# Moving the last transfer of a cached-attention decode kernel, and the wait for it, from SyncE to ScalarE

## The chip, the cores and the metric

The kernel runs on one core of one Trainium2 chip. The metric is device microseconds (us) of that core for one execution. Times of several executions are given as medians.

Each engine of the core runs its own program. In this kernel TensorE does the matmuls, VectorE and ScalarE the elementwise work, and SyncE nothing but issue transfers and wait; they wait for one another by counters, called semaphores. Its matmul results lie in PSUM, everything else that it keeps on the core in SBUF. The instruction that starts a transfer shows in the trace as its **issue slice**; the bytes move afterwards, in packets, through the 16 transfer (DMA) engines that the profile counts.

Two quantities are used beside the time: the **span**, which the profile gives for an execution (first recorded instruction to last), and the time less the span of the same execution, called **time past the span** below. The span is listed to 0.1 us for each run, so a single time past the span is good to 0.05 us only, and means carry more than single values.

## The reference

One token (x has 512 elements) goes through layer norm, attention over a cache of 65536 positions (32 query heads, 8 key/value heads of width 128), the output projection, then a gated feed-forward of width 1792.

```python
def _A_ref(x, k_cache, v_cache, wq, wo):
    q = (x @ wq).reshape(B, Sq, Hq, Dh)...          # cut
    scores = jnp.einsum("bhqd,bhkd->bhqk", q, k) * (Dh ** -0.5)
    p = _softmax(scores, axis=-1)
    o = jnp.einsum("bhqk,bhkd->bhqd", p, v)
    return o...reshape(B, Sq, Hq * Dh) @ wo         # cut

h  = x + _A_ref(_layernorm(x), A_k_cache, A_v_cache, A_wq, A_wo)
h2 = h + ((_sigmoid(g) * u) @ w_down)               # g, u from layernorm(h) @ w_gate, w_up
return h2                                           # 1 x 1 x 512, bfloat16
```

The two caches are 2 x 8 x 65536 x 128 bfloat16 elements, 268 MB of the 282 MB that are read. The output is one row of 1 KB.

## The kernel before

A small class records the instructions of each engine with what they depend on, gives each engine a semaphore, each stream of transfers another, and emits one program per engine. The parts that matter:

```python
def dma(self, eng, fn, sem, deps=(), name=None):      # a transfer adds 16 to its own semaphore when it has landed
    self.op(eng, fn, deps, name)
    ...

HINTED = ("pe", "dve", "act")    # these three programs lie in a loop that is never repeated
def hinted(e, eng):
    ...
    with self.nc.body(first, valid_engines=here):
        loc = eng.mark_branch_hint_location()
        run(e, eng)
        eng.br_lt(never, 1, on_true=first, on_false=end).branch_hint(loc)     # L189
    self.nc.switch_bb(end)

for e, eng in (("sp", nc.sync), ("pool", nc.gpsimd), ("act", nc.scalar), ("dve", nc.vector), ("pe", nc.tensor)):
    ...
    (hinted if e in HINTED else run)(e, eng)
    nc.br("fin", engines=here)                        # every engine leaves its own program here
nc.switch_bb("fin")
for sem, v, _ in (value[d] for d in self.at_end):
    nc.sync.wait_ge(sem, v)                           # L211: the last wait of the kernel
```

SyncE issues all loads but that of x, each when its place is free (for nearly all of them a slot in a ring of four of 4 MB). The last of them are the three pieces of w_down. Then comes the end:

```python
# 56 matmuls (L831) leave the output in PSUM, a quarter each on rows 0, 32, 64, 96 of one bank
for g in (0, 2, 1, 3):
    if g < 2:   # VectorE
        op("dve", lambda e, g=g: e.tensor_copy(y_sb[:, 128*g:128*g+128], ps(YB, 0, 128, 32*g, 32*g+1)), ["y"], f"ysb{g}")
    else:       # ScalarE
        op("act", lambda e, g=g: e.activation(y_sb[:, 128*g:128*g+128], ps(YB, 0, 128, 32*g, 32*g+1), AF.Copy), ["y"], f"ysb{g}")
dma("sp", lambda e: e.dma_start(out[0], y_sb[:, :]), "out", [f"ysb{g}" for g in range(4)], "out")    # L841
P.at_end = ("out",)
```

## Time and profile before

| | before |
|---|---|
| time, median | 658.1 us (3 runs); 658.24 with the 3 taken beside the changed kernel |
| span of the profiled execution | 657.1 us |
| read from HBM | 282.33 MB, 430 GB/s over the span |
| last matmul ends | 655.26 us |
| last copy of the output ends | 655.90 |
| output issued, packet moves, wait over | 655.96, 656.71, 657.10 |

The lines behind this table stand in the prediction. The table is read from the bottom up: a change of the last transfer can act on the 1.2 us after the last copy. Everything else is a stream of loads, and time that a transfer engine loses in the stream is lost at the end too (run j below measures it: 0.27 us for each of eight added packets of 0.31).

### The profile page before, as it was taken

To read this page: it belongs to the slowest core of one execution; us is meant where nothing else is said; L and a number is where in the kernel's file an instruction comes from. 1 tells how busy PE (TensorE), PEld (TensorE's weight loads), DVE (VectorE), ACT (ScalarE), POOL (GpSimd) and SP (SyncE) were. 2 spreads that over 40 slices of the span, in tenths; PEclk is the share of its full clock that TensorE was granted. 3 is DMA by queue.
4 is the path that set the end of the run, shared out by engine and by line. 5 is a ranking of instruction groups with operands and counts; after the bars stand their busy time and mean duration, and the time that the engine had idled before them with its cause. 6 is when DMAs were issued, how large, how long until landed. Compare 5 with 4: busy or idle time off the path is not lost. (4 is left out here: it accounts for less than half of the span.)

```text
span 657.1 us, 6111 instructions
## 1 busy us (share of the span) xinstructions
PE 420.5 (64%) x2315; PEld 74.1 (11%) x1547; DVE 349.7 (53%) x439; ACT 42.9 (7%) x114; POOL 3.6 (1%) x17
## 2 busy tenths in 40 slices
PE   0688488548666585576765575764866668556746
PEld 0200011011000010010100110101100001001322
DVE  2399775547537665347555374465743575542202
ACT  1100200020000200020000200002000100002001
POOL 1000000000000000000000000000000000000000
PEclk9989689677888697776966769765888869677676
DMA  9999999999999999999999999999999999999998
GB/s 383 447 433 429 439 423 431 431 447 415 447 415 447 437 425 447 415 447 419 443 441 421 447 415 447 423 439 443 419 447 415 447 427 435 445 417 427 435 430 352
DMA packets 10802, 282.34 MB, mean 430 GB/s; under 512 B 1329, under 2 KB 1330, under 8 KB 1842
## 3 DMA queue, kind: packets, MB, share of 16 engines
q1 hardware_dynamic: 10658, 282.33, 99.7%
q10 hardware_dynamic: 144, 0.00, 0.0%
HBM read 282.33 MB, written 0.00 MB: 430 GB/s over the span
## 5 line engine op out<-in xcount | busy, mean ns | idle before, releaser
L431 PE MATMUL PS<-ktw 128*128 128x512 bf16 x1024 | 299.9, 442 | 157.4 <-DVE ktw L511 153.6
L511 DVE STREAM_TRANSPOSE ktw<-ring 128x1024 f32<-128x1024 f32 x256 | 291.6, 1205 | 128.0 <-DMA ring<-in_A_k_cache_dram 128.0
L431 PE MATMUL PS<-ring,PT_sb 128*32 x1024 | 83.9, 455 | 23.6 <-issue 13.2
L431 PEld LDWEIGHTS PS<-ktw 128*128 x256 | 27.1, 106 | 408.2 <-issue 256.8
L565 DVE STREAM_TRANSPOSE PT_sb<-P_sb 128x512 bf16<-128x512 bf16 x32 | 20.2, 684 | 54.0 <-PE PS L602 52.3
L551 ACT ACTIVATE negmax<-PS 128x1 f32<-128x1 f32 x8 | 1.4, 171 | 520.6 <-PE PS L549 520.6
L431 PEld LDWEIGHTS PS<-ring,PT_sb 128*32 x1024 | 25.8, 116 | 79.8 <-issue 74.6
L516 DVE TENSOR_REDUCE M_sb<-PS 128x1 f32<-128x512 f32 x32 | 19.9, 684 | 25.5 <-PE PS L431 25.5
L555 ACT ACTIVATE P_sb<-PS,negmax 128x512 bf16<-128x512 f32 x32 | 21.6, 686 | 0.3
L572 DVE TENSOR_REDUCE lsum<-PS 128x1 f32<-128x4 f32 x8 | 1.3, 163 | 31.2 <-PE PS L570 31.2
L542 PE MATMUL PS<-identf,gm 128*1 128x128 f32 x16 | 3.4, 301 | 16.9 <-DVE gm L540 16.9
L616 DVE TENSOR_TENSOR Lw<-O,blk_of 128x896 bf16<-128x896 bf16 (+1 forms) x2 | 1.4, 683 | 20.6 <-ACT O L606 20.6
L402 PE MATMUL PS<-st,onesf 128*128 128x2 f32 x4 | 1.2, 362 | 16.1 <-DVE st L401 16.1
L431 PE MATMUL PS<-ring,xz 128*8 x32 | 9.2, 459 | 2.3 <-issue 2.3
L599 ACT ACTIVATE po_sb<-PS,rl 128x512 bf16<-128x512 f32 x8 | 5.5, 687 | 53.2 <-PE PS L431 53.2
L431 PE MATMUL PS<-ktw,O 128*1 x26 | 7.6, 464 | 0.0
L549 PE MATMUL PS<-one_f,gmrep 1*128 1x1 f32 x16 | 4.2, 330 | 5.0 <-DVE gmrep L546 5.0
L555 ACT ACTIVATION_READ_ACCUMULATOR P_sb<-PS,negmax 128x1 f32 x32 | 6.5, 202 | 0.0
L476 DVE STREAM_TRANSPOSE qt<-qh 32x512 bf16<-32x512 bf16 x1 | 0.7, 699 | 10.6 <-ACT qh L473 10.6
L602 PE MATMUL PS<-sel_bf,po_sb 128*128 128x4 bf16 x32 | 2.0, 168 | 6.4 <-ACT po_sb L599 6.4
L417 DVE CAST hT<-x_col 128x4 f32<-128x4 bf16 x1 | 0.2, 171 | 10.6 <-DMA x_col<-in_A_x_dram 10.6
L661 DVE COPY yr<-PS 1x512 f32<-1x512 f32 x1 | 0.7, 679 | 8.3 <-PE PS L659 8.3
(82 smaller groups left out, 74.0 us busy)
## 6 DMA issues: line engine op xcount, KB each, us to landing
ring<-in_A_k_cache_dram SPq DMA_DIRECT2D x32, 4096.0 KB, 28.7
ring<-in_A_v_cache_dram SPq DMA_DIRECT2D x31, 4096.0 KB, 26.4
ring<-in_A_wq_dram SPq DMA_DIRECT2D x1, 4096.0 KB, 12.3
ktw<-in_A_wo_dram SPq DMA_DIRECT2D x1, 3584.0 KB, 12.7
ring<-in_A_v_cache_dram SPq DMA_DIRECT2D x1, 3072.0 KB, 13.2
ring<-in_B_w_gate_dram SPq DMA_DIRECT2D x1, 1792.0 KB, 19.0
ring<-in_B_w_up_dram SPq DMA_DIRECT2D x1, 1344.0 KB, 21.7
ring<-in_A_v_cache_dram SPq DMA_DIRECT2D x1, 1024.0 KB, 15.2
```

Of the source, the lines that this page charges most:

```text
L431: return e.add_instruction(mybir.InstMatmult(name=nc.get_next_instruction_name(), engine=mybir.EngineType.PE, ins=[rhs, lhsT], outs=[e.low ...
L511: op("dve", lambda e, d=dst, sr=src: e.transpose(d, sr), deps, f"T{b}.{c}", to="T")
L516: op("dve", lambda e, u=u: e.tensor_reduce(M_sb[:, u % 4:u % 4 + 1], ps(u % NS, 0, 512), AX.X, ALU.max), [f"S{b}.{NC - NR + k}"], f"mx{u}" ...
L542: op("pe", lambda e: e.matmul(ps(MISC, 0, 128, 0, 1), lhsT=gm[:, :], rhs=identf[:, :], start=True, stop=True), [f"gm{h}"], f"gmT{h}", to="Q")
L549: op("pe", lambda e: e.matmul(ps(MISC, 128, 129), lhsT=gmrep[0:1, :], rhs=one_f[0:1, 0:1], start=True, stop=True), [f"gmrep{h}"], f"neg{h}")
L551: op("act", lambda e: e.activation(negmax[:, k:k + 1], ps(MISC, 128, 129), AF.Copy, scale=-att_scale), [f"neg{h}"], f"negmax{h}")
L555: op("act", lambda e, b=b: e.activation(P_sb[:, (b % 4) * 512:(b % 4 + 1) * 512], ps(b % NS, 0, 512), AF.Exp, bias=negmax[:, k:k + 1], sca ...
L565: op("dve", lambda e, b=b: e.transpose(PT_sb[:, (b % 4) * 512:(b % 4 + 1) * 512], P_sb[:, (b % 4) * 512:(b % 4 + 1) * 512]), [f"E{b}", f"o ...
L572: op("dve", lambda e: e.tensor_reduce(lsum[:, :], ps(MISC, 132, 136), AX.X, ALU.add), [f"l{h}"], f"ls{h}", to="D")
L599: op("act", lambda e: e.activation(po_sb[:, :], ps(PO, 0, 512), AF.Copy, scale=rl[:, :]), [f"PV{NR * h + NR - 1}", f"rl{h}"], f"po{h}", to ...
L602: op("pe", lambda e, t=t: e.matmul(ps(OX, 0, 4), lhsT=po_sb[:, t * 128:(t + 1) * 128], rhs=sel_bf[:, 8 * t:8 * t + 8:2], start=(t == 0), s ...
L616: op("dve", lambda e: e.tensor_tensor(Lw[i][:, :].rearrange("p (j c) -> p j c", j=n), bass.AP(tensor=O2, offset=j0, ap=[[NQ, 128], [1, n], ...
```

## The change

The intent: the engine that makes half of the last copies issues the transfer itself and waits for it, so that SyncE is not woken across engines at the very end.

```diff
         for sem, v, _ in (value[d] for d in self.at_end):
-            nc.sync.wait_ge(sem, v)
+            nc.scalar.wait_ge(sem, v)
...
-        dma("sp", lambda e: e.dma_start(out[0], y_sb[:, :]), "out", [f"ysb{g}" for g in range(4)], "out")
+        dma("act", lambda e: e.dma_start(out[0], y_sb[:, :]), "out", [f"ysb{g}" for g in range(4)], "out")
```

## The prediction

> **What bounds the kernel now.** I read the page of the profile from the top, then the chain of waits and the timeline of the last microseconds, then the waits of the queue that issues the transfers. The page first:
>
> ```profile
> span 657.1 us, 6111 instructions
> PE 420.5 (64%) x2315; PEld 74.1 (11%) x1547; DVE 349.7 (53%) x439; ACT 42.9 (7%) x114; POOL 3.6 (1%) x17
> DMA  9999999999999999999999999999999999999998
> DMA packets 10802, 282.34 MB, mean 430 GB/s; under 512 B 1329, under 2 KB 1330, under 8 KB 1842
> q1 hardware_dynamic: 10658, 282.33, 99.7%
> q10 hardware_dynamic: 144, 0.00, 0.0%
> ```
>
> The reader is to see that the DMA row is full from the first slice on (only the last, with the tail in it, has 8): 282.34 MB at 430 GB/s is 656.6 us, the span itself. No compute engine is above 64%. The kernel streams the two caches and the weights, and only what lies after the last byte has arrived is not streaming. All but a sliver goes through queue 1, fed by SyncE; queue 10 has 144 packets, which is the load of x issued by ScalarE (128 rows and 16 small packets more). The output goes through queue 1 now. So the change touches the last piece of the span and nothing of the stream; the share of ScalarE's busy time (7%) says nothing about it.
>
> The last piece is in the timeline of the end (columns: start us, us, engine, line, operation, tiles, count, idle time before and what ended it):
>
> ```profile
> 653.58 1.68 PE L831 MATMUL PS<-ring,hhT 128*1 128x128 bf16 x56 [0.98 <-DVE hhT L826]
> 655.31 0.57 ACT L839 ACTIVATE y_sb<-PS 1x128 bf16<-1x128 f32 x2 [4.23 <-PE PS L831]
> 655.31 0.59 DVE L837 CAST y_sb<-PS 1x128 bf16<-1x128 f32 x2 [1.78 <-PE PS L831]
> 655.96 0.33 SPq L841 DMA_DIRECT2D out_dram<-y_sb  x1
> ```
>
> and in the waits of SyncE's queue from 600 us on (columns: engine and line, what it waited for, total us, times, longest):
>
> ```profile
> SPq L120 <- ACT y_sb L839: 25.9, 1, 25.9
> SPq L365 <- PE PS L431: 14.8, 2, 8.0
> SPq L362 <- PE PS L431: 11.1, 1, 11.1
> SPq L211 <- DMA out_dram<-y_sb: 0.8, 1, 0.8
> ```
>
> Here one sees the whole tail. The last matmuls end at 655.26. ScalarE and VectorE each copy two quarters of the output row out of PSUM, to 655.88 and 655.90. SyncE has stood waiting for 25.9 us (so its last weight load was issued by about 630), issues the output at 655.96, is busy with the issue for 0.33, until 656.29, and waits 0.8 more, to 657.1, where the span ends. From the last copy to the end it is 657.1 - 655.90 = 1.2 us: 0.06 from the copy to the issue, 0.33 of issue, 0.8 of flight and receipt. That 1.2 us is 0.18% of the time, and it is the most that any form of this change could remove. In the records of the transfers the one packet of 1 KB moves at about 656.71, some 0.75 us after the issue starts, so about 0.4 us of the wait is the way back to the waiting engine.
>
> **What the Trainium skill says.** "DMA: Bandwidth & Descriptors", section "SWDGE vs HWDGE vs iDMA", states that a transfer issued by ScalarE takes the same hardware descriptor path as one issued by SyncE, and its section "Issuing engines are not separate DMA queues" that they end on the same 16 engines, so that another issuer saves only sequencer time. The trace of before agrees as far as it goes: the issue of x on ScalarE took 375 ns; SyncE's issues were 327 to 501 ns (median 328) for the K loads, 419 to 432 for the closely following w_down loads, 326 for the output. "Perfetto Trace Analysis", section "Per-engine timelines", says that data movement is outside the issue's slice and that a write to HBM can hold up the final semaphore; the 0.8 us of waiting after a 0.33 us slice, with no other traffic, agrees. "Runtime: NRT & Kernel Launch", section "The ~15µs preamble/postamble breakdown", gives about 5 us of barrier and reset after the kernel; the measured 658.1 is only 1.0 above the profiled span of 657.1 (two executions, so not exactly comparable), so that work can't all be in the metric. The same page, section "Instruction fetch mechanics", warns that a taken branch can stall on the fetch of its target. This I take up as a rival.
>
> **The change, part by part.**
>
> *The issue moves to ScalarE.* One instruction leaves SyncE's program and one enters ScalarE's. It still depends on the four copies. Two are ScalarE's own, two VectorE's. A copy's completion must still be waited for even by the engine that made it, since the transfer reads the bytes from SBUF: there is a semaphore wait either way. What might be gained is the hop from ScalarE to SyncE, but VectorE's copies end last (655.90 against 655.88) and their hop remains, to another listener. So the start of issue stays at about 655.96: at best 0.02 earlier, if the sequencer's waits are in another order 0.03 to 0.05 later.
>
> Is ScalarE's sequencer there in time? The records of its loop-closing branch say so: ScalarE ran the branch of L189 at 655.3, for 53 ns, while its copies were still to be executed. The sequencer runs ahead of its engine, so it will already be standing at the wait when the copies end, as SyncE does now.
>
> *The duration of the issue.* SyncE took 326 ns. ScalarE's only sample is 375, but it ran at 0.80 while SyncE was also issuing at 0.81, and SyncE's own closely spaced issues are slower too. Nobody else issues at the end. I take 326 to 375, thus 0 to +0.05 us.
>
> *Flight and receipt.* Same 1 KB, same single packet, same destination, all weight traffic over (the last of it at 654.6, with no more packets before the output's): 0.8 us, change 0. Queue 10 is empty, but so is queue 1 by then, so there's nothing to overtake.
>
> *ScalarE's branches.* After the issue ScalarE must run the compare-and-branch (53 ns) and a jump before it reaches the final wait. This lies beside the 0.8 us of flight: 0 on the path.
>
> *SyncE is freed.* It ends at about 630 instead of 657.1. It would only have waited; the stream of loads is issued in the same order at the same times. 0.
>
> Sum: -0.02 to +0.05 at the start, 0 to +0.05 in the issue, 0 in flight, 0 in the end wait: between -0.02 and +0.10 us of 658.1, some 0.015% at the most. Three runs of before span 0.16 us, so this is under the noise.
>
> **The rivals.**
>
> *The output is held up on ScalarE.* If the sequencer could not process the transfer until the engine's own queue is drained, or the branch to the common end block stalls on instruction fetch for longer than the 0.8 us of flight, the end moves later. For it: after the change the path out of ScalarE's hinted loop is on the engine that decides the end, before it was not. Against: the branch now takes 53 ns, and up to 0.8 us of any stall is hidden. It would make 658.4 to 659.5.
>
> *The hop is real and saved.* If most of the 0.06 us between copy and issue, and part of the 0.4 us on the way back to the waiter, belong to SyncE rather than to the memory, ScalarE may do both faster. For it: the change has one engine that copies, issues and waits. Against: half of the copies are on VectorE, and the way back comes from the transfer, whoever listens. It would make 657.8 to 658.0.
>
> *The end of the program has another order.* SyncE can reach the closing barrier 27 us early and ScalarE is last. If what is measured past the span (1.0 us) includes a hand-over from engine to engine, it may shift by a few tenths either way: 657.7 to 658.5. Nothing in the trace speaks to its sign.
>
> *The stream is disturbed.* No load changes issuer or order, and the queue's share is full in 39 of 40 slices. I give this nearly nothing. A whole-run shift of over 0.3% could only come from another state of the chip.
>
> **Range and chances.** The centre is 658.1, the old median plus about 0.03. The 80% range is the third rival's width, a little wider to the side of the first: 657.7 to 658.6. For 2% it would take 13.2 us, eleven times the whole 1.2 us tail: faster is excluded by the profile (0.005 is for the measurement), slower is nearly so (0.005, a bad state or an unforeseen stall).
>
> **What would show it.** In the changed profile the transfer should be in ScalarE's queue at 655.9 to 656.0 relative to a tail like this one (0.05 to 0.11 us after the last copy), 0.33 to 0.38 long, the end wait of L211 with ScalarE as the waiter and 0.7 to 0.9 us, and q10 with 146 packets, q1 two fewer (10656). The DMA row, 430 GB/s and the K and V issues unchanged. It would be wrong if the gap from last copy to issue grew beyond 0.2 us, if the issue lasted over 0.5, or if the end wait grew to over 1 us; a change in the time without any of these would be the third rival.

## The result, and the profile after

658.54 us (median of 6, 658.4 to 658.81) against 658.24 (6 runs, 658.04 to 658.39). The ratio is 1.0005, 95% interval 0.9993 to 1.0018: the same. A ratio compares the means of the runs of the two kernels, not the medians quoted beside it (the ratios come out when the first execution of each kernel, the profiled one, is left out).

The end of the changed kernel, as the timeline has it (start us, us, engine, line, operation, tiles, count, idle time before and what ended it), and after it the one line for the final wait (L211, by engine, with its duration in ns and its start):

```profile
655.07 0.34 PE L831 MATMUL PS<-ring,hhT 128*1 128x128 bf16 x8 [0.23 <-DMA ring<-in_B_w_down_dram]
655.45 0.59 DVE L837 CAST y_sb<-PS 1x128 bf16<-1x128 f32 x2 [1.71 <-PE PS L831]
655.45 0.56 ACT L839 ACTIVATE y_sb<-PS 1x128 bf16<-1x128 f32 x2 [3.96 <-PE PS L831]
656.10 0.51 ACTq L841 DMA_DIRECT2D out_dram<-y_sb  x1
```

```profile
L211 ACTq EVENT_SEMAPHORE  x1: 17/17/17, 657.2 to 657.2; - x1
```

From the last copy (656.04) to the issue it is 0.06 us as before. The issue takes 0.51 instead of 0.33. Yet in the records the packet moves at 656.85, 0.75 us after the issue starts, exactly as before, and the wait is over 1.15 us after the issue starts, against 1.14. So the tail after the last copy is 1.21 us against 1.20, and the longer issue isn't in it. What the tail doesn't hold must lie above it or past the span. In this trace the last matmuls waited 0.23 us for w_down, where in the trace of before they waited for VectorE alone; but this isn't the mark of the change: the traces of k and g below have the same wait (0.23 and 0.24) with nothing new in the stream, and one of the changed kernel (l) doesn't have it.

The queues, from the page of the changed kernel:

```profile
DMA packets 10803, 282.34 MB, mean 430 GB/s; under 512 B 1329, under 2 KB 1330, under 8 KB 1842
q1 hardware_dynamic: 10656, 282.33, 99.7%
q10 hardware_dynamic: 146, 0.00, 0.0%
q14 instruction: 1, 0.01, 0.0%
```

Queue 1 has two packets less and queue 10 two more, as predicted. But the total is 10803, not 10802: a packet of an instruction queue now lies inside the span. The records give it 8 KB, a start at 634.2 us and 309 ns. In the kernel before there is one like it, outside the span: 0.3 us after its end, at 657.4. The same part of the two traces, first the changed kernel from 633.5 to 635, then the kernel before from 657 to 659:

```profile
DMA packets 22, 0.52 MB, mean 350 GB/s; under 512 B 0, under 2 KB 0, under 8 KB 0
q1 hardware_dynamic: 21, 0.52, 81.0%
q14 instruction: 1, 0.01, 1.3%
```

```profile
DMA packets 2, 0.02 MB, mean 12 GB/s; under 512 B 0, under 2 KB 0, under 8 KB 0
q8 instruction: 1, 0.02, 3.8%
q14 instruction: 1, 0.01, 1.1%
```

SyncE issued its last load until 630.6 us in the changed kernel and then left its program; 3.6 us later this packet moves among the last weights. In the kernel before SyncE leaves at 656.3, after the issue of the output, and the packet moves 1.1 us later. So there is a suspect that the prediction had not looked for. The small difference of the medians, 0.3 us, can have three parts: the issue, the stream, and what is measured past the span.

### The profile page after: what moved, and what is told of

Read it like the earlier page. It is cut to its first block, busy times and chain, and to the rows that moved or that the text cites. A ratio compares the mean times of both kernels' runs of the same rounds, so it can differ in the third digit from the quotient of the medians.

```text
span 657.3 us, 6111 instructions
## 1 busy us (share of the span) xinstructions
PE 419.9 (64%) x2315; PEld 73.6 (11%) x1547; DVE 349.7 (53%) x439; ACT 42.9 (7%) x114; POOL 3.6 (1%) x17
## 2 busy tenths in 40 slices
DMA packets 10803, 282.34 MB, mean 430 GB/s; under 512 B 1329, under 2 KB 1330, under 8 KB 1842
```

## The experiments

Twelve kernels were run, in three calls of four; those of one call shared a chip and nine executions of the kernel before. Every kernel gave a right result.

### Halves of the change (first call)

The kernel before once more, and the changed kernel once more, without edits:

> The kernel before itself, for its spans: only its time and one profiled span are known so far (658.2 and 657.1). Tail from the last copy to the end 1.20 us, issue slice 0.33, time ratio 1.000. Quantity of interest: measured time less span. Hand-over theory (who ends last decides what is measured past the span): about 1.1 us here, against 1.45 in the runs of the changed kernel. Issue theory (ScalarE's longer issue slice, 0.51 against 0.33, is the cost) and noise theory: about 1.45 here as well.

> The changed kernel again on this chip. All theories: issue slice on ScalarE about 0.51 us. Issue theory: tail from last copy to end 1.2 + 0.19 = 1.4 us. Hand-over theory: tail 1.2 us and time less span about 1.45 us, 0.3 over the kernel before. Noise theory: tail 1.2, and no difference in time to the control beyond 0.1 us.

SyncE issues, ScalarE waits:

```diff
-            nc.sync.wait_ge(sem, v)
+            nc.scalar.wait_ge(sem, v)
```

> SyncE issues, ScalarE alone waits at the end: half of the change. Issue theory: as the kernel before, 658.2. Hand-over theory: as the changed kernel, about 0.3 us slower than before, time less span about 1.45, with a tail of 1.2 us. Noise theory: no difference.

ScalarE issues, SyncE waits:

```diff
-        dma("sp", lambda e: e.dma_start(out[0], y_sb[:, :]), "out", ...
+        dma("act", lambda e: e.dma_start(out[0], y_sb[:, :]), "out", ...
```

> ScalarE issues, SyncE waits at the end: the other half. Issue theory: as the changed kernel, about 0.2 to 0.3 us slower than before. Hand-over theory: as the kernel before, time less span about 1.1 us. Noise theory: no difference. All: issue slice about 0.51 us; the packet moves 0.75 us after the issue starts.

| kernel (5 runs each) | ratio to before, 95% | median us | mean span | past the span, least / median | tail after last copy | issue slice | instruction packet (8 KB) at |
|---|---|---|---|---|---|---|---|
| a: before | 0.9999 (0.9985 to 1.0012) | 658.17 | 656.84 | 1.34 / 1.37 | 1.21 | 0.326 | 657.04, after the end |
| b: changed | 1.0010 (0.9996 to 1.0023) | 658.76 | 657.14 | 1.46 / 1.46 | 1.20 | 0.513 | 633.88 |
| c: SyncE issues, ScalarE waits | 1.0009 (0.9996 to 1.0023) | 658.78 | 656.88 | 1.46 / 1.78 | 1.21 | 0.326 | 657.30, after the end |
| d: ScalarE issues, SyncE waits | 1.0011 (0.9998 to 1.0025) | 659.06 | 657.06 | 1.31 / 2.06 | 1.21 | 0.514 | 633.87 |

The kernel before in the same call: median 658.30, mean span 656.90, past the span 1.33 / 1.39.

No time is clear of noise at this size; all four are the same. The parts are clearer than the sum. The issue theory falls: the tail is 1.20 to 1.21 us in all four traces, whichever engine issues, and the 0.19 us that the slice is longer do not appear in it. The noise theory, as I put it for the control (1.45 us past the span there too), misses, and so does the hand-over theory's 1.1: the control has 1.37. My 1.1 came from setting the median time beside a span of another execution; that profiled execution took 659.41 us itself.

What remains splits the change in two. Where ScalarE issues, the mean span is 0.2 longer and the instruction packet lies in the stream (b, d). Where ScalarE waits, no run has less than 1.46 us past the span (b, c), where SyncE waits the least is 1.31 to 1.34. And single runs in all kinds take up to 1.7 us more past the span (c has 3.10 once, the kernel before 1.95 once); these set the medians of c and d, and nothing in the traces shows why.

### The issue and the landing, multiplied (second call)

Seventeen output transfers in a row, each issued when the one before has landed:

```diff
-        dma("sp", lambda e: e.dma_start(out[0], y_sb[:, :]), "out", [f"ysb{g}" for g in range(4)], "out")
-        P.at_end = ("out",)
+        engines = ["sp"] * 17                 # f: ["act"] * 17, and ScalarE waits at the end
+        for i, eng in enumerate(engines):     # g: ["sp", "act"] * 8 + ["sp"]
+            dma(eng, lambda e: e.dma_start(out[0], y_sb[:, :]), "out",
+                [f"out{i - 1}"] if i else [f"ysb{g}" for g in range(4)], f"out{i}")
+        P.at_end = (f"out{len(engines) - 1}",)
```

> Seventeen output transfers one after the other, each issued by SyncE after the one before has landed (same bytes, right result): 16 more links than the kernel before. In the single transfer a link is 1.14 us from issue to release of the waiter, so all theories expect 16 x 1.15 = 18 us more: about 676.7.

> The same chain with every issue and wait on ScalarE. Theory A (the longer issue slice of ScalarE, 0.51 against 0.33, lies beside the flight): the same 1.15 us per link, within 0.5 us of the SyncE chain. Theory B (the longer issue slice or ScalarE's own handling is on the path of a transfer): 16 x 0.19 = 3 us more than the SyncE chain.

> The chain with SyncE and ScalarE issuing in turn, so that each link's landing is waited for by the engine that did not issue it. Theory A: who waits makes no difference to the landing, 1.15 us per link as in the other two. Theory C (an engine sees its own transfer's landing sooner than another engine's, the hop that the change is meant to save): longer than both chains by 16 times the hop, 1 us or more in all if the hop is over 0.06.

| chain (4 runs each) | ratio to before, 95% | mean span | links of the profiled execution, first / later |
|---|---|---|---|
| e: SyncE | 1.0271 (1.0255 to 1.0286) | 674.60 | 1.145 / 1.09 to 1.12, one 1.21 |
| f: ScalarE | 1.0271 (1.0256 to 1.0287) | 674.85 | 1.143 / 1.11 to 1.12 |
| g: in turn | 1.0266 (1.0251 to 1.0282) | 674.70 | 1.146 / 1.10 to 1.14, one 1.22 |

The issues of the three chains, by line and engine (duration in ns, least / median / most; first and last start), e first, then f, then g:

```profile
L843 SPq DMA_DIRECT2D out_dram<-y_sb x17: 227/227/327, 655.8 to 673.5; - x17
```

```profile
L843 ACTq DMA_DIRECT2D out_dram<-y_sb x17: 233/234/507, 656.0 to 673.9; - x17
```

```profile
L843 SPq DMA_DIRECT2D out_dram<-y_sb x9: 227/227/327, 655.6 to 673.5; - x9
L843 ACTq DMA_DIRECT2D out_dram<-y_sb x8: 233/234/508, 656.7 to 672.3; - x8
```

All three are 17.6 to 17.9 us longer in span than the kernel before in the same call (656.96), as 16 links of 1.11 us make; 18 was expected. Theory B, 3 us more on ScalarE, is refuted: the mean spans differ by 0.25. (Even that may not be the chain's: in f SyncE is done early, as in the changed kernel, and the 8 KB instruction packet moves in the stream at 633.9; in e and g it moves in the tail.) Theory C is refuted too: where each landing is seen by the other engine (g), a link is no longer. The long slice of 0.51 us is that of the first issue only; the next ones on the same engine take 0.234, and SyncE's go from 0.327 to 0.227 likewise. The first link is as long on ScalarE (1.143, slice 507 ns) as on SyncE (1.145, slice 327 ns), since the slice goes on beside the flight of the packet. The long single links in e and g, by about 0.1 us, are those during which the instruction packet moves (at 658.5 and 659.2). In e, from 658 to 659:

```profile
q14 instruction: 1, 0.01, 1.9%
q1 hardware_dynamic: 2, 0.00, 0.4%
```

The two packets of the output moved at their usual time in these links (the first 0.70 and 0.72 us after the issue), and SyncE was the one to wait, so the 0.1 us may be the packet's or SyncE's own. Note for what follows that here the packet moves while SyncE still has 14 (e) and 7 (g) transfers to issue: it does not need SyncE to leave its program, only to get on in it.

The fourth kernel of the call made a third engine wait, `nc.vector.wait_ge(sem, v)` in place of `nc.sync.wait_ge(sem, v)`:

> SyncE issues as before, VectorE alone waits at the end: a third engine for the last wait. Hand-over theory (the time past the span depends on which engine ends last: its floor was 1.31 to 1.41 us where SyncE ended, 1.44 to 1.46 where ScalarE did): a floor that differs from SyncE's by about 0.1 us. Noise theory: the same floor as the kernel before in the same rounds, within 0.05.

It is the same as before (1.0000, 0.9986 to 1.0013; mean span 656.88), with 1.38 us as the least past the span, where the kernel before has 1.35 in the same rounds. So in the least value VectorE ending last is within 0.05 of SyncE ending last, as the noise theory had it, and of the three engines only ScalarE shows the 0.1 us. This rests on two of five runs (1.38, 1.39); the median of the five is 1.46.

### The instruction packet (third call)

The changed kernel, with SyncE held in its program until the copies are done:

```diff
         dma("act", lambda e: e.dma_start(out[0], y_sb[:, :]), "out", [f"ysb{g}" for g in range(4)], "out")
+        op("sp", lambda e: None, [f"ysb{g}" for g in range(4)])      # the waits alone, no instruction
```

> The changed kernel, but SyncE still waits for the four copies before it leaves its program (it issues and waits for nothing after that). So far the mean span is 656.90 where SyncE issues the output (33 runs) and 657.10 where ScalarE does (16 runs), though the tail after the last copy is 1.20 to 1.21 us in both. Fetch theory: where SyncE leaves early, 4 us after its last weight load, an 8 KiB packet of the instruction queue (309 ns) is moved in the middle of the last loads instead of 0.3 us after the end; it delays one of the 16 transfer engines and the last weights by up to 0.3 us. It expects the fetch back at about 1.1 us after SyncE leaves, beyond the copies, and a mean span of 656.9. Rival (ScalarE's issue or the placement of its code is the cause, or chance): 657.1, as the changed kernel.

> The changed kernel on the same chip as the others of this call. Fetch theory and its rival: mean span 657.1 against 656.9 of the kernel before, instruction packet at about 634 us. Chance: no difference between the mean spans. Time past the span: at least 1.44 us where ScalarE waits last, as in all 11 runs so far, against at least 1.33 in the kernel before.

The kernel before, with eight loads of one row added (the last is waited for before the tanh, since the program must not end before they have landed):

```diff
+        junk = sb("junk", [1, 4096], bf16)
...
         def head_out(h):
+            dma("act", lambda e: e.dma_start(junk[:, :], A_k_cache[0, h:h + 1, 0:32, :].rearrange("o t d -> o (t d)")), "junk",
+                [f"junk{h - 1}"] if h else (), f"junk{h}")
...
-        ... scale=rstd[1][:, 0:1]), ["gu0", "rstd.1"], "sg")
+        ... scale=rstd[1][:, 0:1]), ["gu0", "rstd.1", f"junk{HKV - 1}"], "sg")
```

> The kernel before with 8 loads of 8 KiB added, one per head, each into one row of an unused tile (so one packet on one of the 16 transfer engines, about as long as the instruction packet), issued by ScalarE in the middle of the stream: 64 KiB more. Fetch theory (a small packet on one transfer engine holds up the stream by its own duration): 8 x 0.31 = 2.5 us more span, if it falls on the same engine each time and nothing catches up. Rival (only the bytes count, the stream catches up): 64 KiB at 430 GB/s = 0.15 us more.

| kernel | runs | ratio to before, 95% | median us | spans of the runs | mean span |
|---|---|---|---|---|---|
| before, same call | 9 | | 658.35 | 656.7 to 657.1 | 656.92 |
| i: changed, SyncE held | 5 | 0.9997 (0.9983 to 1.0010) | 658.33 | 656.7, 656.8, 656.7, 656.9, 656.7 | 656.76 |
| l: changed | 5 | 1.0002 (0.9988 to 1.0016) | 658.89 | 657.1, 657.0, 657.1, 656.9, 657.4 | 657.10 |
| j: before and 8 row loads | 4 | 1.0029 (1.0013 to 1.0044) | 660.48 | 659.1, 659.1, 659.0, 659.2 | 659.10 |

In kernel i nothing of the instruction queues is left between 633.5 and 635; queue 1 is all there is:

```profile
DMA packets 27, 0.66 MB, mean 442 GB/s; under 512 B 0, under 2 KB 0, under 8 KB 0
q1 hardware_dynamic: 27, 0.66, 102.6%
```

and between 655.9 and 656.7 of the same trace, beside the output's two packets on queue 10, it is back, 1.1 us after SyncE's wait was over (655.5):

```profile
q8 instruction: 1, 0.02, 7.2%
q14 instruction: 1, 0.01, 3.4%
q10 hardware_dynamic: 2, 0.00, 0.4%
```

ScalarE issues and waits here just as in the changed kernel, with the same slice (0.512) and the same tail (1.21), and the mean span is 0.34 us shorter and back at that of the kernel before (or a little under it). So it is SyncE's getting on early, not ScalarE's issuing, that lengthened the span. All calls together say the same: 657.10 over 21 runs in which SyncE is through with its program early (the changed kernel and d) against 656.89 over 47 in which it is held to the end (the kernel before, a, c, h, i; not k, whose tail is another), 0.21 with a standard error of 0.04. What goes with it in the records is the instruction packet: in the stream, at 633.8 to 634.2, in all five traces of the first kind (the changed kernel three times, d, and the chain f), and beyond the loads in all others. That it is the packet that costs the time was not shown by moving the packet alone; it is argued from run j.

Kernel j tests whether one such packet could cost that much. Its page shows 16 packets more on queue 10 than the 144 of before, thus two for each load, one of 8 KB and one for the semaphore:

```profile
q10 hardware_dynamic: 160, 0.07, 0.0%
```

The 8 KB packets took 309 ns each in the records, like the instruction packet. The span grew by 659.10 - 656.92 = 2.2 us for eight of them, 0.27 each. If only the bytes counted, it would have been 0.15 in all. So the stream does not catch up: here each such packet cost most of its own duration at the end. The trace shows where. In kernel j, from 655.2 to 656.5, when every load of the kernel before had long landed (654.6 in its trace), 13 packets were still moving, one after the other:

```profile
DMA packets 13, 0.03 MB, mean 25 GB/s; under 512 B 1, under 2 KB 1, under 8 KB 13
q1 hardware_dynamic: 13, 0.03, 6.3%
```

6.3% is one sixteenth: by this share (the records don't name the engine) one of the 16 transfer engines was still working through its part of w_down while the others had finished, and the end waited for it. So the packets fell on the same engine and added up; what a single one costs, on an engine that need not be the last, this does not measure. In the changed kernel no such lag stands out: the last semaphore packet of the loads comes 0.25 to 0.60 us after the median of the last 16 in the five traces with the instruction packet in the stream, and 0.09 to 0.45 us in the eight others without added loads, so the two overlap.

Last, a version aimed at what the tail does hold, one copy of all rows in place of two in a row on each engine:

```diff
-        y_sb = sb("y_sb", [1, D], bf16)
+        y_sb = sb("y_sb", [128, 128], bf16)
...
-        (the four copies, two on VectorE and two on ScalarE)
+        op("dve", lambda e: e.tensor_copy(y_sb[:, :], ps(YB, 0, 128)), ["y"], "ysb")
+        dma("sp", lambda e: e.dma_start(out[0].rearrange("o (g n) -> (o g) n", g=4),
+                                        bass.AP(tensor=y_sb, offset=0, ap=[[32 * 128, 4], [1, 128]])), "out", ["ysb"], "out")
```

> The kernel before with the four copies of the output replaced by one copy of 128 partitions on VectorE, and the transfer reading four of its rows; SyncE issues and waits. A version aimed at what the tail does hold: two copies in a row took 0.59 us, one should take 0.28, so 0.3 us off the piece from last matmul to issue, if the four-row transfer lands as fast as the one-row one (1.14 us). Span 656.6 in the mean. If four rows of 256 bytes cost a longer issue or landing, up to 0.3 us is given back.

```profile
654.77 0.29 DVE L835 CAST y_sb<-PS 128x128 bf16<-128x128 f32 x1 [1.60 <-PE PS L831]
655.09 0.65 SPq L836 DMA_DIRECT2D out_dram<-y_sb  x1
```

The copies shrank from 0.59 to 0.29 us, and more than that was given back (2.06 us from the last matmul to the end of the span, 1.86 before): the issue took 0.65 us, the first of four packets moved 1.25 us after the issue started (0.75 before), and the wait was over after 1.68 (1.14 before). Mean span 657.00 against 656.92, ratio 1.0000 (0.9986 to 1.0013). A 16 KB instruction packet (the q8 one) moved in this time too, but it does so in the tail of run a as well, where the output's packet moved after the usual 0.75, so it is not the likely cause. Whether the cost lies in four rows or in rows of 256 bytes was not separated.

## Why the prediction was right or wrong

**The whole.** The profile bounded the change from above: 1.2 us of tail in 658 us of streaming. That decided the class, and it held. The range held with some luck: 658.54 lies within 657.7 to 658.6, but 0.06 under its end, and the changed kernel taken again had medians of 658.76 (b) and 658.89 (l), above it. Its sum of -0.02 to +0.10 us did not hold. Over all runs with a listed span (32 of before, 16 of the changed kernel), the mean span is 656.91 against 657.11, so +0.20, with a standard deviation of 0.17 in each group and thus about 0.05 on the difference; the median time past the span is 1.40 against 1.49.

**"The issue moves to ScalarE": right.** Copy to issue 0.06 us in both. One point behind it was off: ScalarE's branch, which I had read as a sign that the sequencer runs ahead (it ran 8 ns after the first of the two copies had started), moved behind the issue (656.6 in the changed kernel), as the order of the program has it; it lay beside the flight, as expected.

**"The duration of the issue", 326 to 375 ns: mis-sized.** It was 512 ns, over the 0.5 that I had named as a sign of being wrong. And the place of that term in the sum was wrong as well: I added it to the path, while the chains show that a longer slice changes nothing before the packet moves, 0.75 us after the start either way. The sizing failed since I took ScalarE's one earlier issue, 375 ns for another transfer, as a measure of this one. In these runs the first issue of a series is the long one (507 then 234 ns on ScalarE, 327 then 227 on SyncE; for the row loads of run j 491 then 230, though they lie 7 to 79 us apart). Why the first is longer, and more so on ScalarE, no run shows.

**"Flight and receipt": right.** 1.14 and 1.15 us from issue to the end of the wait, and 1.09 to 1.15 in 49 of 51 links, on either engine and across them. As the slice was longer, the wait after it was shorter, 0.64 us from its end, not 0.7 to 0.9.

**"SyncE is freed ... 0": this is the step that failed.** With it failed the dismissal of the last rival, that the stream is disturbed. I argued that no load changes issuer or order, which is true. But an engine that gets on in its program also has more code fetched, and the profile counts that packet among those of the 16 transfer engines. "Runtime: NRT & Kernel Launch", section "Instruction fetch mechanics", says that the sequencer fetches its next page through a queue of its own; I used that section only for a stall of ScalarE's branch. Run i shows that SyncE's early leaving costs span (0.34 us between l and i, 0.2 over all runs), and run j that one of eight packets of that size, in loads, costs 0.27; that it is the same cost is argued. That the instruction packet is SyncE's is inferred from its time: it came about 1.1 us after SyncE had passed its last issue or wait where nothing else was moving, 3.6 to 4.2 us after its last issue where the queues were full, and within SyncE's chain in e and g.

**"The end of the program has another order": real, about 0.1 us.** All 30 runs in which ScalarE waited last (b, c, f, i, l and the first six) have at least 1.43 us past the span; the kernels in which SyncE waited last have runs down to 1.28 to 1.35, and VectorE's down to 1.38. Nothing in a trace shows what is measured there, so its cause stays open, like that of the single runs with 0.2 to 1.7 us more.

**"The hop is real and saved": refuted** by the alternating chain. In the tail it made no difference over about 0.02 us a link which engine listens.

Together: +0.20 in the span and +0.09 past it, over all runs, make up the +0.3 by which the first medians differ. Both are under what the times alone can separate (the ratio's interval is 0.0025 wide, 1.6 us), and were found only because the spans of many runs could be averaged and the cost multiplied.

## What to carry to other kernels

First bound a change by the piece of the span that it can reach; here that alone gave the right class. Then ask of every engine that the change sets free what it does next: in this kernel, bound by its transfers, letting SyncE get on 26 us early cost 0.2 us, most likely because the code that it goes on to comes through the same transfer engines. A longer slice of an issue need not be a longer transfer: measure from the start of the issue to the packet and to the release of the wait, and multiply a cost by a chain when it is smaller than the noise.

## What the Trainium skill lacked or had wrong

- "Runtime: NRT & Kernel Launch", section "Instruction fetch mechanics", calls the cost of crossing into a next block mostly hidden, and gives blocks of 16 KB. Here an 8 KB packet of an instruction queue (309 ns; others of 16 KB were seen) moved in the stream when SyncE left its program early, and the span was 0.2 to 0.3 us longer; held back until after the loads it cost nothing that shows in the span. The page doesn't say that a stream limited by the transfer engines pays for it.
- "DMA: Bandwidth & Descriptors", section "Issuing engines are not separate DMA queues", is borne out for the transfer itself: 1.11 us a link on ScalarE, 1.10 on SyncE. No page that I read has the duration of the issue slice, nor that the first one is longer: 507 then 234 ns on ScalarE, 327 then 227 ns on SyncE.
- The same page, section "Anatomy of one DMA — SWDGE (gpsimd) path", fits a fixed cost of about 2.0 us per transfer. That is for transfers issued by GpSimd; for the 1 KB row written to HBM from SyncE or ScalarE the runs show 1.14 us, and 1.68 us for the same bytes as four rows of 256 bytes. No page that I read has the whole time from issue to the release of the waiter for a transfer issued by these engines.
- No page has what the measured time holds past the span (1.40 us in the median with SyncE last, 1.49 with ScalarE last).
